# Scores by halves of 128 tokens instead of by even and odd tokens, with a new order list, in a fused recurrent-attention and bilinear feed-forward kernel

## The chip, the cores and the metric

The kernel runs on one core of a Trainium2 chip, in one launch. Time is device microseconds of one run; the median of three runs before the change is 193.85 us (193.69 to 193.97). TensorE (PE) multiplies, VectorE (DVE), ScalarE (ACT) and GpSimd (POOL) work element by element, SyncE (SP) and POOL issue nearly all transfers. Every engine takes its own instructions in the order in which they were written.

## The reference

Inputs are float32: q, k, v and alpha of 4 batches x 8 heads x 768 tokens x 48, and three weights (384x1536, 384x1536, 1536x384). A state of 48x48 per batch and head decays and grows with every token; its outputs, laid side by side over the heads, go through a bilinear feed-forward.

```python
for t in range(S):
    state = alpha[:, :, t, :, None] * state + np.einsum('bhd,bhe->bhde', k[:, :, t], v[:, :, t])
    y[:, :, t] = np.einsum('bhd,bhde->bhe', q[:, :, t], state)
...
x = y.transpose(0, 2, 1, 3).reshape(B * S, H * D)
a = x @ w_a
b = x @ w_b
return (a * b @ w_out)
```

## The kernel before

**Tiling.** A chunk is two batches (u = 0, 1) of 256 tokens; there are six (chunk c has stage c // 2 and batches c % 2 * 2 and the next). Partition p holds the token pair 2p and 2p+1 (r = 0, 1). Partitions 0 to 63 are group g = 0, 128 tokens, and 64 to 127 are g = 1. Within a group outputs come from scores (query times key, masked so that no query sees a later key); between groups and stages a state is carried (Sm, S0).

**Steps of a chunk.** Logarithms of alpha (`ln`, L556) are summed along tokens by PE (`B`, `A2` or `AQ`), ACT takes their exponentials (`E`), DVE scales keys and queries into QKp (`mk`, `mq`, L678; `lv` before them multiplies one token of each pair into the level of the other, L652, and `l2`, `l2s`, `R`, `H`, `L` prepare the sums). QKp is transposed into kqT: in chunks 0 and 1 by PE into PSUM (`C`, L736) and an eviction (`Ce`, L742, L744), from chunk 2 on by one transfer of SP for each batch (`T`, L767). `v` (vcast, L785, L787) copies the values into vxs, spaced by zeros. `K`, `K2` (L799, L812) make the states' growth, `k` (L826 to L830) adds it, `dk`, `de` or `dr`, `dl` bring the decay.

`D` (scores, L841) multiplies keys by queries. For each batch and half of the heads (h) it has 16 matmuls: per pair of heads and per key parity rk, 64 keys on the weights' side (even or odd tokens of a group) and 128 queries streamed. The four matmuls of both groups and both heads of a pair use the four quarters of PE's array together. `M` (L846) masks from PSUM into m, or `Mc` (L850, ACT) copies and `Mm` (L854, DVE) masks in place. `Y` (inner, L865) multiplies values by masked scores, 48 matmuls for a batch, again four side by side; `SB` and `SA` add what the states carry. `X` (evac, L900 on ACT, L902 on DVE) evicts a batch's y of both groups, 768 columns, to xT with the columns in the order (parity, pair). `a` and `b` (ff, L919) multiply xT by 128 columns of w_a or w_b, three matmuls for all 512 tokens of a chunk (`*`) or for 256 (0 or 1); `as` (L925, ACT) evicts a, `pr` (L933, DVE) multiplies it by b out of PSUM and puts the tokens back in their order. `o` (L941) and `oc` (L952) are the last product, `ot` evicts it, `st` stores it.

**Order.** PROGRAM (L17 to L401) is a list of such steps, chunk number first. The loop at its end (L1063 to L1068) calls them one by one, so an engine's instructions follow in the list's order. An entry's last letter is its engine (V = DVE, S = ACT, P = POOL, Y = SP), and a number for a PE step is its PSUM bank out of eight. `ld` loads, `W` and `Wo` load weights (all on POOL), `cz`, `cs`, `cm` set constants on POOL. Transfers issued by POOL take its time in line with the rest of its work. Input tiles have two buffers each, kqT and m have four, `as` three.

Of the kernel before, what the change touches and what calls it, by code (L numbers as in the profile page):

```python
# [9 lines left out]
BF16 = mybir.dt.bfloat16  # L10
# [7 lines left out]
0: cm 0; c1; cz 0 b P; ci; ld a 0b Y; c1a; ld a 0a Y; ln 0b; cu; cz 1 b P; fill 7 2; cu2 V; cz 0 q V; cus; ld k 0b Y; ld k 0a Y; B 0b 5; ld q 0b Y; ld v 0 P  # L18
0: ln 0a; ld q 0a Y; E 0b b; E 0b i; mq 0b V; B 0a 0; E 0a i; dk 0 2; E 0a b; ld a 1 P; mk 0b V; C 0 1 5; cs 0 m P; ld k 1 P; ld q 1 P; v 0 S; mk 0a V; cm 1
0: de 0; fill 2 1; mq 0a V; C 0 0 3; Ce 0 1 V; W b 0 256; cz 0 v P; Ce 0 0 V; D 0 1 4; ln 1; ld v 1 P; W a 256 768; K 0 0 6; k 0 0 V; M 0 1; D 0 0 0; SB 0 6  # L20
0: cz 1 q P; B 1a 2; M 0 0; W a 0 256; E 1a i; E 1a b; W b 256 768; mq 1a V; mk 1a V; B 1b 4; dk 1 3; E 1b i; E 1b b; de 1; v 1 S; mq 1b V; mk 1b V; C 1 0 0
0: Y 0; SA 0; Ce 1 0 V; cs 1 m P
1: ld a 0 P; ld a 1 P
0: W a 768 1536; C 1 1 1; X 0 S; c2 P; D 1 0 3; W b 768 1536
1: ld q 0 P
0: Ce 1 1 V; K 1 0 5; k 1 0 V; a 4 0 0
1: ld k 0 P
0: D 1 1 6; SB 1 1
1: ld v 0 P; ld q 1 P
0: Mc 1 0; a 3 0 5; Wo 0 6; a 0 0 3; Mm 1 0 V; Mc 1 1; as 0 0; b 0 0 4  # L30
1: ld k 1 P
0: pr 0 0; b 1 0 6; a 2 0 3; a 1 0 7; a 5 0 4; as 2 0; b 2 0 3; Mm 1 1 V; as 1 0; b 4 0 7; as 5 0; b 5 0 4; pr 2 0; pr 1 0
1: ln 0
0: SA 1; Y 1; Wo 6 12; K 1 1 6; as 3 0; as 4 0; X 1 S
1: ra 0
0: K 0 1 3
1: l2 0 V
0: b 3 0 0; pr 5 0; pr 4 0
1: H 0 V; L 0 V
0: a 2 1 1; a 5 1 2; as 5 1; pr 3 0; a 1 1 7; b 4 1 5; b 5 1 4; as 2 1; k 0 1 V; pr 5 1; a 4 1 2; as 1 1  # L40
1: ln 1
0: b 2 1 0; pr 2 1; a 6 * 3; as 4 1; b 1 1 2
1: l2 1 V
0: pr 4 1; as 6 *
1: H 1 V
0: pr 1 1
1: A2 0 7
0: a 11 * 0; a 7 * 5; a 0 1 4
1: L 1 V
0: k 1 1 V  # L50
1: ra 1
0: as 11 *
1: lv 0 q V; E 0 i
0: as 0 1; b 6 * 0; b 11 * 3; a 8 * 4; pr 6 *; pr 11 *
2: ld a * P
0: b 0 1 1; as 8 *; a 3 1 6
1: E 0 b; lv 0 k V
0: a 10 * 2; pr 0 1
1: mq 0 V; ld v 1 P
0: b 8 * 4  # L60
1: A2 1 7
0: as 10 *; b 10 * 2; pr 8 *
1: E 1 b
0: as 3 1; as 7 *; b 9 * 3; b 3 1 0; b 7 * 1; a 9 * 6
2: ld q * P
1: v 0 S; lv 1 q V; mk 0 V
0: pr 10 *
1: mq 1 V; C 0 1 4
0: as 9 *
1: C 0 0 2  # L70
0: o 0 0 5; pr 7 *
1: dk * 6
2: ld k * P
3: ld v * P
0: cz 1 v P; pr 9 *
1: Ce 0 0 S; E 1 i; de *; lv 1 k P; Ce 0 1 V; D 0 1 1; D 0 0 3
0: pr 3 1
1: Mc 0 0; K2 0 0 7 0
0: o 1 0 6
1: mk 1 V; M 0 1  # L80
0: o 3 0 4; o 1 1 -; ot 1 S; c3 P
3: ld a * P
0: cs 1 0 P; o 3 1 -
1: k 0 0 V; k 0 1 V; Mm 0 0 V; SB 0 1; C 1 0 3; C 1 1 7
0: ot 3 S; o 0 1 -
1: Ce 1 0 V
2: ln *
1: v 1 V; D 1 0 3; Ce 1 1 S; K2 1 1 6 0; Y 0; SA 0
0: ot 0 V
# [12 lines left out]
1: as 2 0
0: ot 2 S
1: pr 4 0
2: R 1; lv 1 q P
1: b 3 0 6; b 2 0 7; a 5 0 2; pr 3 0; b 5 0 3; as 5 0; b 1 0 5; a 1 0 1; pr 5 0; pr 2 0; a 7 0 2; as 1 0; pr 1 0
2: AQ 3
1: SB 1 6
2: lv 0 k P
1: a 10 0 5  # L110
2: lv 1 k V; ra 0; ld v * P
1: Mm 1 1 V
2: E 1 b
1: as 10 0; b 10 0 0; pr 10 0
2: mq 1 V; E 1 i
1: as 7 0; b 7 0 1
2: E 0 b; E 0 i
1: a 0 0 5
0: st 3 Y
2: dr  # L120
1: SA 1; Y 1
2: mk 1 V
1: pr 7 0; a 11 0 0; a 6 0 3; b 6 0 2; X 1 S; b 11 0 4; a 2 1 6; as 6 0; a 3 1 7; as 11 0; b 2 1 1; pr 6 0
2: lv 0 q V
1: b 4 1 0; as 2 1
2: T 1
1: pr 11 0
2: dl
0: st 0 Y
1: a 0 1 2; pr 2 1  # L130
2: mq 0 V
1: b 3 1 3; b 0 0 6; as 3 1; as 0 0; b 0 1 7; pr 3 1; a 8 0 1; a 9 0 5
0: st 1 Y
1: b 8 0 3; b 9 0 4; pr 0 0; as 0 1
2: mk 0 V
1: a 4 1 2
3: ln *
1: a 9 1 6; pr 0 1; as 8 0; b 9 1 1
3: ra 1
1: b 10 1 7; pr 8 0; a 10 1 3; as 4 1; as 9 0; as 9 1; a 6 1 6; b 6 1 2; b 11 1 5; pr 4 1; as 10 1; pr 9 0; a 11 1 4; pr 10 1; pr 9 1; as 6 1  # L140
2: v 1 S
1: a 8 1 3; b 8 1 1; a 7 1 6; pr 6 1
3: l2 0 V
1: as 11 1
2: T 0
1: as 8 1; a 5 1 4
3: ra 0
1: as 5 1; a 1 1 2
2: v 0 V
4: ld a * Y  # L150
1: pr 11 1; as 7 1; pr 8 1
2: K2 * * 0 7; D 1 1 3; D 1 0 5
1: as 1 1; b 5 1 2; o 2 0 1
2: k * 0 V
1: pr 5 1
3: v 0 S; v 1 S
1: b 1 1 2
2: Mc 1 0; M 1 1
3: l2s 0 P; l2s 1 P
1: b 7 1 0; o 2 1 -; pr 1 1; o 3 0 4  # L160
2: SB 0 5
# [216 lines left out]
5: b 11 * 1
# [26 lines left out]
def kernel(  # L405
# [160 lines left out]
    def bank(i):  # L566
        return psum[:, int(i)]
# [531 lines left out]
```

## Time and profile before

| | us |
|---|---|
| median of 3 runs | 193.85 (193.69 to 193.97) |
| span of the profiled execution | 192.0 |
| PE busy | 186.8 |
| DVE busy | 133.1 |
| ACT busy | 106.5 |
| POOL busy | 56.9 |
| first feed-forward matmul starts | 18.3 |
| last matmul's piece of the chain ends | 188.66 |

The span runs from the first to the last instruction; the runs' times also hold what lies around it. Matmuls are pipelined, so the mean duration of one in the profile (216 to 379 ns) is a latency; how fast they follow one another is read from their starts. PE's clock was granted in full. Lines of helpers are told apart by what they read and write.

### The profile page before, as it was taken

What the parts mean: (1) busy time and instruction counts of PE and PEld (TensorE: products, weight loads), DVE (VectorE), ACT (ScalarE), POOL (GpSimd) and SP (SyncE); (2) the same over time, 40 slices, a digit from 0 to 9 for tenths busy, and PEclk for the clock granted to TensorE, in tenths of its full rate; (3) what the DMA queues carried; (4) which work ended last, traced back from release to release, by engine and by line L of the source; (5) the groups of instructions that cost most, each with busy time, mean ns of one, the idle gap of its engine ahead of it and who ended that gap; (6) DMA issues with size and microseconds to landing.
All of it is one profiled execution on the core that took longest, in us unless ns stands there. A gap on an engine that the chain in (4) does not pass through costs nothing.

```text
span 192.0 us, 6086 instructions
## 1 busy us (share of the span) xinstructions
PE 186.8 (97%) x2613; PEld 116.9 (61%) x2613; DVE 133.1 (69%) x223; ACT 106.5 (55%) x194; POOL 56.9 (30%) x75
## 2 busy tenths in 40 slices
PE   7999999999999999999999999999999999999992
PEld 3888875677778876645557444656465644545562
DVE  2387698994989888899897956887567446252510
ACT  4448885656779867753487756743572435314211
POOL 8999626752450500640074262000000000000000
PEclk9999999999999999999999999999999999999999
DMA  5999999999969999999999989017641200000422
GB/s 132 274 219 218 251 253 235 244 269 264 251 107 166 165 216 265 248 254 149 233 213 181 156 174 129 3 42 140 146 66 44 85 0 0 0 0 3 164 82 82
DMA packets 62618, 29.40 MB, mean 153 GB/s; under 512 B 53712, under 2 KB 60768, under 8 KB 62592
## 3 DMA queue, kind: packets, MB, share of 16 engines
q0 software_dynamic: 18432, 13.37, 39.6%
q1 hardware_dynamic: 44016, 15.55, 38.1%
q8 instruction: 20, 0.33, 0.7%
q10 hardware_dynamic: 144, 0.10, 0.2%
q14 instruction: 6, 0.05, 0.1%
HBM read 25.98 MB, written 4.74 MB: 160 GB/s over the span
## 4 chain that ended last, share of the span: by engine, by line
PE 91%; DMA 5%; SPq 1%; DVE 1%; issue 1%; ACT 0%; DVEq 0%
PE psum L919 47%; PE psum L941 24%; PE psum L865 7%; PE psum L841 3%; DMA kqT<-QKp 3%; DMA q_t<-in_q_dram 3%; PE psum L736 2%; PE psum L633 1%; PE psum L952 1%; SPq L549 1%; PE psum L799 1%; PE psum L812 1%; PE psum L700 1%; PE psum L591 1%; PE psum L592 1%
## 5 line engine op out<-in xcount | busy, mean ns | idle before, releaser
L919 PE MATMUL psum<-xT,wb_t 128*128 128x512 bf16 (+1 forms) x270 | 56.0, 337 | 0.0
L919 PE MATMUL psum<-xT,wa_t 128*128 128x512 bf16 (+1 forms) x270 | 56.0, 337 | 0.0
L941 PE MATMUL psum<-wo_t,prod 128*128 128x384 bf16 x276 | 49.4, 326 | 0.0
L919 PEld LDWEIGHTS <-wb_t 128*128 128x128 bf16 x270 | 25.9, 98 | 19.9 <-issue 0.5
L919 PEld LDWEIGHTS <-wa_t 128*128 128x128 bf16 x270 | 25.9, 98 | 19.7 <-issue 0.3
L941 PEld LDWEIGHTS <-prod 128*128 128x128 bf16 x276 | 25.9, 98 | 17.6
L956 ACT ACTIVATE ot<-psum 128x384 f32<-128x384 f32 (+1 forms) x16 | 7.7, 482 | 22.7 <-PE psum L941 21.6
L850 ACT ACTIVATE m<-psum 128x1024 bf16<-128x1024 f32 x14 | 14.1, 1023 | 4.6 <-PE psum L841 4.3
L613 POOL TENSOR_TENSOR l<-la 64x384 f32<-64x384 f32 x7 | 7.8, 1108 | 26.6 <-ACT la L556 19.0
L846 DVE TENSOR_TENSOR m<-psum,mask 128x1024 bf16<-128x1024 f32 x10 | 12.1, 1220 | 3.1 <-PE psum L841 3.1
L652 POOL TENSOR_TENSOR q_t<-q_t,ra 128x384 f32<-128x384 f32 x5 | 6.1, 1215 | 22.5 <-ACT ra L645 19.7
L556 ACT ACTIVATE la<-a_t 128x1536 f32<-128x1536 f32 (+2 forms) x9 | 9.5, 1055 | 2.3 <-DMA a_t<-in_alpha_dram 2.2
L678 DVE TENSOR_TENSOR QKp<-q_t,beta 128x768 bf16<-128x768 f32 x10 | 10.0, 995 | 1.0 <-ACT beta L667 1.0
L865 PE MATMUL psum<-m,vx 64*64 64x128 bf16 x576 | 10.5, 217 | 0.0
L900 ACT ACTIVATE xT<-psum 128x768 bf16<-128x768 f32 x9 | 7.2, 816 | 5.7 <-PE psum L865 5.5
L678 DVE TENSOR_TENSOR QKp<-k_t,invb 128x768 bf16<-128x768 f32 x10 | 9.7, 972 | 0.8 <-ACT invb L667 0.8
L854 DVE TENSOR_TENSOR m<-m,mask 128x1024 bf16<-128x1024 bf16 x14 | 9.3, 684 | 1.2 <-ACT m L850 1.2
L958 DVE COPY ot<-psum 128x384 f32<-128x384 f32 (+1 forms) x9 | 4.8, 532 | 7.6 <-PE psum L941 4.7
L865 PEld LDWEIGHTS <-vx 64*64 64x64 bf16 x576 | 9.0, 107 | 0.5 <-issue 0.3
L841 PE MATMUL psum<-kqT 64*64 64x128 bf16 x384 | 9.0, 219 | 0.4 <-DMA kqT<-QKp 0.3
L652 POOL TENSOR_TENSOR k_t<-k_t,a_t 128x384 f32<-128x384 f32 x6 | 7.4, 1228 | 6.1 <-issue 3.3
L549 POOL DMA_DIRECT2D v_t<-in_v_dram x8 | 8.5, 1058 | 0.1
(271 smaller groups left out, 287.9 us busy)
## 6 DMA issues: line engine op xcount, KB each, us to landing
out_dram<-ot SPq DMA_DIRECT2D x23, 192.0 KB, 3.8
q_t<-in_q_dram SPq DMA_DIRECT2D x3, 768.0 KB, 6.5
a_t<-in_alpha_dram POOLq DMA_DIRECT2D x2, 768.0 KB, 15.2
k_t<-in_k_dram POOLq DMA_DIRECT2D x2, 768.0 KB, 12.1
v_t<-in_v_dram POOLq DMA_DIRECT2D x4, 384.0 KB, 7.0
a_t<-in_alpha_dram SPq DMA_DIRECT2D x2, 768.0 KB
k_t<-in_k_dram SPq DMA_DIRECT2D x2, 768.0 KB
a_t<-in_alpha_dram POOLq DMA_DIRECT2D x3, 384.0 KB, 8.5
```

What stands on the lines that cost most here:

```text
L549: eng.dma_start(out=t[:, us, hs].rearrange("p b h r d -> p (b h) (r d)"), in_=src[ch.b0 + us.start:ch.b0 + us.stop, hs, ch.s * 2 * C:(ch.s ...
L556: nc.scalar.activation(out=ch.la[:, us, hs].rearrange("p b h r d -> p (b h r d)"), in_=ch.a[:, us, hs].rearrange("p b h r d -> p (b h r d) ...
L613: eng.tensor_add(ch.l2[(1 - g) * HC:(2 - g) * HC, 1], x[:, :, 0, :], x[:, :, 1, :])
L652: eng.tensor_mul(x, x, by)
L678: eng.tensor_mul(QKp[ch.c % 2][:, u, j, :, hs, :D], src[:, u, hs].rearrange("p h r d -> p r h d"), f)
L841: nc.tensor.matmul(s2[g * HC:(g + 1) * HC, r, p, rk, :], lhsT=turned_part(ch, u, 1, rk, 2 * h + p, g, rs), rhs=queriesT(ch, u, 2 * h + p, ...
L846: nc.vector.tensor_mul(m.rearrange("p r a k s -> p (r a) (k s)"), ch.s2[u, h].rearrange("p r a k s -> p (r a) (k s)"), maskn(4))
L850: nc.scalar.activation(out=m.rearrange("p r a k s -> p (r a) (k s)"), in_=ch.s2[u, h].rearrange("p r a k s -> p (r a) (k s)"), func=AF.Copy)
L854: eng.tensor_mul(x, x, maskn(4))
L865: nc.tensor.matmul(y[c * DP:(c + 1) * DP, g, j // 2 * C:(j // 2 + 1) * C], lhsT=lhsT, rhs=rhs, start=(g, c) not in begun, stop=False, skip ...
L919: nc.tensor.matmul(p, lhsT=(wa_t, wb_t)[w][:, kk, f * 128:(f + 1) * 128], rhs=ch.xT[:, kk, us, :], start=(kk == 0), stop=(kk == KT - 1))
L941: nc.tensor.matmul(op, lhsT=ch.prod[:, f, at:at + C], rhs=wo_t[:, f, :], start=(f == 0), stop=(f == NFF - 1))
```

## The change

Scores are taken by the first and the last 64 tokens of a group (x = 0, 1) instead of by parity. Keys of the last 64 meet only the last 64 queries, so those matmuls stream 64 columns. m has 192 columns where it had 256, and the mask likewise. For that the 64 keys on the weights' side have to lie together. In chunks 0 and 1 PE's transposes write them so in PSUM and the eviction copies straight. From chunk 2 on a new step `Tr` (turn_keys) copies the transposed keys into a tile kp of three buffers, on ACT or DVE.

The values' rows have to stand in the same order of tokens. Half of them do already after `v`; the other half moves by 32 partitions in a new step `vs` (vswap): for a batch and a group two copies of 32 partitions x 384 elements, 13 of the 24 steps on DVE, 7 on ACT, 4 on POOL. The states' growth (`K`, `K2`) reads the loaded v instead of vxs. `X` works on one group at a time (384 columns, 10 on DVE, 14 on ACT; before it were 3 and 9 of 768) and puts the tokens in order, so that `pr` writes contiguously. The number of matmuls stays.

The whole list is new. By engine, before and after: `Ce` on DVE 6 and 4, on ACT 2 and 4; `v` on DVE 3 and 6, on ACT 9 and 6; `lv` on POOL 11 and 7, on DVE 9 and 13; `l2s` on POOL 7 and 3, on DVE 1 and 5; `l2` on DVE 6 and 5, on POOL none and 1; `ot` and `otc` on DVE 9 and 10, on ACT 16 and 15. The list's start, and the place about the middle of chunk 2, in the new order:

```
+0: C 0 0 0; Ce 0 0 V; Ce 0 1 S; ld q 1 P; K 0 0 2; de 0; k 0 0 V; D 0 1 4; ln 1; cm 1; D 0 0 0; M 0 0; W b 0 256; SB 0 2; v 0 S; vs 0 0 P; B 1a 6; E 1a b
+0: E 1a i; B 1b 0; dk 1 6; M 0 1; cz 0 v P; vs 0 1 V; Y 0; ld v 1 P; mq 1a V; mk 1a V; C 1 0 7; E 1b b; mq 1b V; W a 256 768; cz 1 q P; E 1b i; mk 1b V; SA 0
+0: X 0 1 V; X 0 0 V; C 1 1 0; Ce 1 1 V; K 0 1 1; de 1; K 1 0 6; k 1 0 V; Ce 1 0 S; D 1 0 4; Mc 1 0; k 0 1 V; b 1 0 2; a 2 0 3; W a 0 256; a 1 0 0; SB 1 4; as 1 0
+0: v 1 V; W b 256 768; as 2 0; Mm 1 0 V; pr 1 0; cs 1 m P
+1: ld a 0 P
+0: vs 1 0 V
+1: ld a 1 P
+0: W a 768 1536; vs 1 1 V; D 1 1 6; a 4 0 1; c2 P; Mc 1 1; Mm 1 1 V; b 5 0 0; b 4 0 3; a 0 0 2; as 0 0; W b 768 1536
...
+2: X 0 0 V; a 4 * 2; b 11 * 0
+3: lv 1 q P
+2: a 11 * 3; as 11 *
+4: lv 0 k V
+3: mk 0 V
+2: a 1 * 6; as 1 *; a 2 * 4
+4: ld q * Y
+2: b 2 * 3; pr 11 *
 1: ot 0 S
+3: mq 0 V; lv 1 k V; E 1 i; mk 1 V
+2: b 1 * 5; pr 1 *; a 3 * 0; a 7 * 1; as 7 *; b 7 * 6; pr 7 *; as 3 *; b 3 * 7; pr 3 *
+3: mq 1 V
+4: ra 1
 1: st 3 Y
+2: as 2 *; pr 2 *
+3: K2 * * 1 5
```

SP's transfers about there, in the old list: `T 0` of chunk 2, `ld a` of 4, `ld q` and `ld k` of 3, `ld k` of 4, a store. In the new one: `T 0` of chunk 2, `ld a` of 4, a store, `ld q` and `ld k` of 3, a store, `ld k` of 4. The functions:

```diff
     def turn(ch, u, h, i):
-        t = ch.tp[u, h] = bank(i).bitcast(BF16).rearrange("p (j r a s) -> p j r a s", j=2, r=2, a=2)
+        ch.tp[u, h] = bank(i).bitcast(BF16)
+        qs = ch.tp[u, h][:, :4 * C].rearrange("p (r a s) -> p a r s", r=2, a=2)
+        ks = ch.tp[u, h][:, 4 * C:].rearrange("p (a q r s) -> p a r q s", r=2, a=2, q=4)
...
-                    nc.tensor.transpose(t[:, j, r, p], QKp[ch.c % 2][:, u, j, r, hp:hp + 2, :].rearrange("s h d -> s (h d)"), ident)
+                    nc.tensor.transpose((ks if j else qs)[:, p, r], QKp[ch.c % 2][:, u, j, r, hp:hp + 2, :].rearrange("s h d -> s (h d)"), ident)
...
+    def turn_keys(ch, u, eng):
+        t = alloc_t(ch, u)
+        x = wk.tile([C, 8 * C], BF16, name="kp", bufs=3)
+        ch.kp[u] = x.rearrange("p (h a q w) -> p h a q w", h=2, a=2, q=4)
+        ch.qT[u] = t[:, :8 * C].rearrange("p (r h a s) -> p h a r s", h=2, a=2, r=2)
+        evict(x.rearrange("p (y r s) -> p y r s", r=2, s=HQ), t[:, 8 * C:].rearrange("p (r y s) -> p y r s", r=2, s=HQ), eng)
...
+    def vswap(ch, us, g, eng):
+        for x in range(2):
+            to, of = (slice(g * HC + n * HQ, g * HC + (n + 1) * HQ) for n in (x, 1 - x))
+            o_ = vxs[ch.c % 2][to, us, 1 - x, :, :D]
+            i_ = ch.v[of, us, :, x, :]
...
+            evict(o_, i_, eng)
...
-                        nc.tensor.matmul(kv[r * DP:(r + 1) * DP, e:e + D], lhsT=QKp[i][gs, u, 1, rk, 2 * p + r, :], rhs=vxs[i][gs, u, rk, 2 * p + r, :D], start=(rk == 0), stop=(rk == 1))
+                        nc.tensor.matmul(kv[r * DP:(r + 1) * DP, e:e + D], lhsT=QKp[i][gs, u, 1, rk, 2 * p + r, :], rhs=ch.v[gs, u, 2 * p + r, rk, :], start=(rk == 0), stop=(rk == 1))
...
+    def cols(x):
+        return slice(x * C, C + x * HC)
...
     def scores(ch, u, h, tag):
...
-            for rk in range(2):
+            for x in range(2):
...
-                        nc.tensor.matmul(s2[g * HC:(g + 1) * HC, r, p, rk, :], lhsT=turned_part(ch, u, 1, rk, 2 * h + p, g, rs),
-                                         rhs=queriesT(ch, u, 2 * h + p, g, rs), start=True, stop=True)
+                        nc.tensor.matmul(s2[g * HC:(g + 1) * HC, r, p, cols(x)], lhsT=keysT(ch, u, 2 * h + p, g, rs, x),
+                                         rhs=queriesT(ch, u, 2 * h + p, g, rs, x), start=True, stop=True)
...
+                        m = ch.m[u, h // 4][gs, h % 2 * 2 + h // 2 % 2, cols(x)].rearrange("p (r s) -> p r s", r=2)
+                        out_mm(ch, u, g, h, j, vx[gs, u, x, at:at + DP], m, x)
...
+    def evac(ch, u, g, eng):
...
+            ch.xT = wk.tile([128, B, KT, C], BF16, name="xT")
+        evict(ch.xT[:, 2 * u + g].rearrange("p a (s r) -> p a r s", r=2),
+              ch.y[u][0][:, g, :KT * C].rearrange("p (a r s) -> p a r s", a=KT, r=2), eng)
...
-            nc.tensor.matmul(p, lhsT=(wa_t, wb_t)[w][:, kk, f * 128:(f + 1) * 128], rhs=ch.xT[:, kk, us, :], start=(kk == 0), stop=(kk == KT - 1))
+            nc.tensor.matmul(p, lhsT=(wa_t, wb_t)[w][:, kk, f * 128:(f + 1) * 128], rhs=ch.xT[:, us, kk, :], start=(kk == 0), stop=(kk == KT - 1))
...
-        o_, a_, b_ = tokens(ch.prod[:, f, :], us), columns(a[:, :n], n), columns(b, n)
-        nc.vector.tensor_mul(o_, a_, b_)
+        nc.vector.tensor_mul(ch.prod[:, f, us.start * C:us.stop * C], a[:, :n], b)
```

More of the change, by code (lines that the diff above doesn't have):

```diff
@@ new lines @@
+0: ot 1 S
+2: l2s 0 V
+1: D 1 1 4; a 4 0 6; as 4 0; a 2 0 7; as 2 0
+2: l2s 1 V; R 0
+1: k 1 0 V; k 1 1 V; a 3 0 3; b 4 0 0; Mc 1 1
+2: R 1
+1: pr 4 0; a 1 0 6
+2: ra 1; lv 1 q P
+1: as 3 0
+0: ot 0 S
+1: a 5 0 7; as 5 0; b 2 0 1; pr 2 0
+2: lv 0 k V
+0: o 2 0 4
+1: SB 1 0
+2: AQ 2
+1: as 1 0
+2: E 1 b; ld v * P
+1: D 1 0 6
+2: lv 1 k P
+1: Mm 1 1 V; b 5 0 5
+2: E 1 i
+0: o 2 1 -
+2: E 0 b
+1: b 9 0 3
+2: dr
+1: M 1 0
+2: ra 0
+1: b 3 0 6; pr 5 0; b 1 0 5; SA 1
+2: mk 1 V
+1: Y 1
+2: E 0 i
+1: a 9 0 2; a 10 0 7; pr 3 0
@@ new lines @@
+1: ot 2 S
+2: D 0 0 4; Mc 0 0; D 1 0 6; Mc 1 0
+3: vs 1 1 S; l2s 0 P
+1: b 3 1 0; pr 3 1; o 0 0 1
+3: l2s 1 P; R 0
+2: SB 0 2
+3: R 1
+2: SB 1 4; D 0 1 6; Mc 0 1; Mm 0 1 V
+0: st 1 Y; cs 0 0 P
+1: o 3 0 0; o 3 1 -
+2: Mm 1 0 V
+4: ln *
+3: AQ 6; E 0 b
+4: l2s 0 P
+3: E 1 b
+2: Y 1
+3: lv 0 k P
+4: ld k * Y
+3: dr
+2: SA 1; X 1 0 S; Mm 0 0 V; Y 0; SA 0
+1: o 0 1 -
+2: X 0 1 S
+1: ot 3 S
+3: lv 0 q P
+2: X 1 1 V
+3: E 0 i
+2: X 0 0 V; a 4 * 2; b 11 * 0
+3: lv 1 q P
+2: a 11 * 3; as 11 *
+4: lv 0 k V
@@ new lines @@
+3: SA 1
+4: vs 0 0 V
+3: Y 1; X 1 1 S; Y 0; X 0 0 S
+2: o 0 0 0; o 0 1 -; o 3 1 -
+5: ln *
+3: X 0 1 V
+4: mk 0 V; T 0
+2: o 1 0 4; o 1 1 -
+3: X 1 0 V; a 0 * 2; a 8 * 3
+4: E 1 b; vs 0 1 V
+3: b 0 * 6
+5: ld k * P
+4: dr; mq 1 V; E 1 i; mk 1 V; T 1
+3: b 2 * 1
+5: l2 0 V
+3: as 0 *
+5: l2s 0 V
+4: vs 1 0 S
+3: b 3 * 2; as 8 *
+5: l2s 1 V; R 0
+4: vs 1 1 S
+3: a 3 * 3; as 3 *
+2: ot 1 S
+5: lv 0 k V
+3: pr 0 *
+1: st 1 Y
+3: b 8 * 6; pr 8 *
+2: ot 3 V
+3: a 2 * 7
+4: dl
+3: as 2 *; a 5 * 3
+4: Tr 0 S
@@ L991, in gate_t @@
     def gate_t(x, u):
[L993 removed]
+        nc.gpsimd.tensor_copy(go, x.kqT[int(u)][0:1, 0:1])
     OPS = {
```

709 lines of the change are left out of this document (281 added, 428 removed).

## Prediction

> **What bounds the kernel now.** I read the page first (totals, then the chain), then the waits of TensorE.
>
> ```profile
> span 192.0 us, 6086 instructions
> PE 186.8 (97%) x2613; PEld 116.9 (61%) x2613; DVE 133.1 (69%) x223; ACT 106.5 (55%) x194; POOL 56.9 (30%) x75
> PE 91%; DMA 5%; SPq 1%; DVE 1%; issue 1%; ACT 0%; DVEq 0%
> ...
> PE psum L574 <- DVE og L472: 1.2, 1, 1.2
> PE psum L841 <- DMA kqT<-QKp: 0.3, 1, 0.3
> PE psum L736 <- DVE QKp L678: 0.2, 1, 0.2
> ```
>
> TensorE (PE) is the chain, and after its first 9 us it waits for 0.3 us in all. So time falls by whatever work leaves PE, as long as every other engine and the loads still keep it fed. Whether they do is the question, for the order list is new from end to end. The chain's last PE piece ends at 188.66; an eviction and a store (3.3 us) follow in both kernels. The span of 192.0 lies 1.85 below the median of 193.85; I sum on the span and add 1.85 at the end. Differences within 0.2% (0.4 us) can't be told from no change.
>
> Two stages of the other engines matter. VectorE (DVE) by stretch (columns: stretch, length, busy and count of each engine):
>
> ```profile
> 40.00:60.00 20.00, 20.00 (x387) 15.18 (x380) 16.03 (x31) 13.82 (x28) 6.84 (x7) 1.00 1.16 207
> 60.00:80.00 20.00, 20.00 (x402) 14.97 (x401) 17.32 (x34) 15.32 (x29) 4.08 (x5) 1.00 1.13 220
> 80.00:110.00 30.00, 30.00 (x414) 16.11 (x413) 27.41 (x37) 18.76 (x32) 11.04 (x9) 1.00 1.05 198
> ```
>
> The third busy column is DVE: 80%, 87%, then 91%. It has little room just where keys, queries and scores of the next chunk are made beside the feed-forward. The other stage is the start, where GpSimd (POOL) issues the loads one behind the other:
>
> ```profile
> 8.50 0.77 POOL L529 DMA_DIRECT2D wb_t<-in_moe_w_b_dram  x1
> 9.32 0.74 POOL L513 MEMSET vx<- 128x768 f32 x1
> 9.99 0.90 POOL L549 DMA_DIRECT2D v_t<-in_v_dram  x1
> 10.88 0.75 POOL L529 DMA_DIRECT2D wa_t<-in_moe_w_a_dram  x1
> ...
> wb_t<-in_moe_w_b_dram POOLq DMA_DIRECT2D x1, 384.0 KB, 7.6
> ...
> v_t<-in_v_dram POOLq DMA_DIRECT2D x1, 192.0 KB, 5.5
> ```
>
> The last two lines are single issues with their us to landing: columns 256 to 768 of w_b (issued 12.86) land at 20.5, v of the second batch (issued 9.99) at 15.5. The transfer engines are full from 5 us on, so what is issued late lands late.
>
> **The change, part by part.** *PE.* Half of the scores' and half of the inner matmuls stream 64 columns instead of 128. They run four at a time, one on each quarter of the array.
>
> ```profile
> L865 PE MATMUL psum<-m,vx 64*64 64x128 bf16 x576 | 10.5, 217 | 0.0
> L841 PE MATMUL psum<-kqT 64*64 64x128 bf16 x384 | 9.0, 219 | 0.4 <-DMA kqT<-QKp 0.3
> ...
> 94.61 0.69 PE L812 MATMUL psum<-vx,QKp 64*64 64x48 bf16 x64
> 95.14 0.40 PE L841 MATMUL psum<-kqT 64*64 64x128 bf16 x16
> ```
>
> The 64 of 48 columns take 0.53 us to the next start: 33 ns for four. Four of 128 columns take 55 to 56 ns (sixteen of L841 hold the chain for 0.22 us at 100.51). For 64 columns the nearer row is 48 columns: 33 ns. Groups of four that become short: (576 + 384)/2/4 = 120. Saving 120 x 23 ns = **2.8 us**; bounds 0 (no faster than 128) and 2.9 (32 ns). The Trainium skill ("TensorE: Matmul & The Clock Gate", section "Wait — 56ns, not 53.3ns?") says that start-to-start never drops below about 25 ns however small a matmul is; then a group of four would take 100 ns and nothing would be saved. The trace disagrees for matmuls on quarters of the array: 8.3 ns each in the row above.
>
> The other matmuls keep their number. Feed-forward reads xT in runs of 128, which costs nothing: L841 already reads its queries in two runs of 64 at full rate.
>
> *DVE.* From 952 ns (xT, 768 elements) and 554 ns (ot, 384) an element of PSUM costs 1.04 ns. Ten M lose 256 elements: -2.7. Fourteen Mm (684 ns) lose a quarter at most, less the fixed part: -1.9. Ninety products write contiguously: 0 to -3, taken -1.5. X: three of 952 become ten of 0.57: +2.8. Thirteen vs, two copies each of 384 bf16 elements: 350 ns for 768 (L787) gives about 250 ns each, +6.5; bounds 4.6 (half of 350) and 14.4 (554, the rate of one element a cycle). Four Tr of 1024: +1.9 (0.35 x 1.33) to +2.8 (0.69). Work that comes over from POOL (four lv, four l2s, less one l2): +4.2; v, Ce, ot together +0.5. Sum about +9 on 133, hidden by the rest of PE's time as a total, but not where DVE stood at 91%.
>
> *ScalarE (ACT)*: 14 copies for vs at 0.49 (ot, 384) and six of 1.02 for Tr and Ce, +13; Mc, v, X and ot give back 6.5. 113 of 192 is hidden. *POOL* loses eight element-wise instructions of 1.1 to 1.2 and gains eight copies.
>
> *The start.* This is the dear part. In the list, POOL's first copy (vs 0 0 P) stands behind W b 0 256 and ahead of cz 0 v, ld v 1 and all further weights. It waits for v 0 on ACT. Before, that cast ran at 9.28. Now it stands behind Ce 0 1 (1.02), de 0 and ln 1, and ln 1 can't start before 10.80, when alpha of the second batch lands (that row stays). 10.80 + 0.84 + 0.84 = 12.4. Two POOL copies at 0.6 each (bounds 0.3, the memset of 256, and 1.2, its multiplies of 384), the memset 0.75: ld v 1 is issued at 14.3 instead of 9.99. By then all earlier loads have landed (W b 0 256 at 8.50 + 5.9 = 14.4), so nothing in the queue covers the gap. A load of two batches of v on an empty queue took 5.7 us (issued 99.37); one batch less 1.1, estimate 4.6: landing 18.9, 3.4 late (bounds 2.4 with quick copies, 4.3 with 5.5). I take 3.3, and the weights behind keep their spacing: w_b 256 to 768 lands at 23.7. The Trainium skill ("GPSIMD Engine Reference", the specifications) says that POOL shares its SBUF interfaces with VectorE; by that each copy could take the 1.2 and the start another 1.2. POOL's multiplies show 0.99 to 1.65 for one size, which agrees.
>
> PE waits meanwhile: first at K 1 0, which now reads v itself, then at a 2 0, a 1 0 and b 5 0. What it has left at b 5 0, against the old kernel where b 3 0 starts at 24.14, 164.5 before the end: seven more feed-forward halves (0.333 each), Y 1, SA 1, K 1 1, together +3.2; short matmuls still to come, -2.3. So PE ends at 23.7 + 164.5 + 0.9 = **189.1** (188.2 to 190.1) against 188.66. Without the gap it would be 185.9. The start eats the saving.
>
> *The middle.* On DVE's list, lv 0 k of chunk 4 now stands right behind the evictions of chunk 2 (free at about 80), ahead of mk 0 of chunk 3 and the product of block 11, whose bank a 3 needs. It waits for chunk 4's k, a load of SyncE (SP):
>
> ```profile
> 63.31 2.84 SPq L767 DMA_TRANSPOSE kqT<-QKp  x1
> 66.26 1.45 SPq L549 DMA_DIRECT2D a_t<-in_alpha_dram  x1
> 67.81 1.27 SPq L549 DMA_DIRECT2D q_t<-in_q_dram  x1
> 69.17 7.47 SPq L549 DMA_DIRECT2D k_t<-in_k_dram  x2
> 76.73 2.78 SPq L974 DMA_DIRECT2D out_dram<-ot  x1
> ```
>
> Four loads of 0.79 MB at the 0.26 MB/us of this stretch end at about 81. In the new list the transpose ahead of them goes about 1 later (0.5 by the list, 0.4 with PE), and two stores of 0.2 MB stand between the loads (1.5): 83.4. Then lv 0.75, mk 0.95, product 0.7: a 3 can start at 85.8. From there PE has 89 blocks of 0.656 (three of L919), 32 halves of the last product at 0.99, four at 0.5 and 10.1 of scores and states left: 102.2, and 1.8% more, by which such a sum fell short of the trace before (161.6 against 164.5 from b 3 0). 189.1 - 104.0 = 85.1. A stall of 0.5 to 0.7, and 0.3 at K2 of chunk 3, whose bank waits for pr 1: **+0.9** (0 to 2.5). Where PE, ACT and DVE hand over closely elsewhere (C 1 1 and Y 0 of chunk 1, SB 0 of chunk 1, X of chunk 2): +0.1 (0 to 1).
>
> Sum: PE ends at 190.1; +3.3 is 193.4; +1.85 is **195.3 us**.
>
> **The rivals.**
> *Faster: the late start is covered.* If v 0 runs ahead of ln 1, or the loads catch up, w_b lands by 21 and PE never waits in the start. Then 2.8 less, about 0.5 lost elsewhere: 191.6. It decides at 23.3 for w_b: earlier than that the start gains. For it: POOL is idle then, and queues that restart empty may land faster than 4.6. Against it: ACT's order is fixed and alpha's landing at 10.8 does not move. Chance 0.20.
> *Only the start costs*: k of chunk 4 lands by 82, DVE keeps up. 189.1 + 3.3 + 1.85 = 194.2, down to 193.4. Chance 0.20.
> *DVE becomes the bound from 40 to 132*: it was busy 77.5 of 92 there; nearly all the additions fall there, 87. If half of its old 14.5 idle stays, because it waits in its order, 87 + 7 = 94: 2 us more than PE has, on top of the start and of the wait for k: 198. For it: 91% in one stretch already. Against it: a late DVE finds its inputs ready. Chance 0.10.
> *The saving isn't there* (short groups take 56 ns, as by the 25 ns rule they would not shrink): 195.3 + 2.8 = 198.1. The row of 48 columns speaks against it. Chance 0.03.
>
> **How the numbers follow.** The forecast holds 0.47, with its own range 194.3 to 197.2. The range is 192.4 to 197.7: the lower end takes in most of the start's good cases, the upper the slow copies on POOL. Faster: 0.20 and a tenth of the second rival, 0.22. Same: most of the rest of that one (193.5 to 194.2), 0.13. Slower: 0.65.
>
> **What would show it.** Groups of four at 33 ns in the short scores and inner matmuls; PE busy less by about 2.8 in work. POOL idle from about 9.3 to 12.4 and ld v 1 issued near 14.3; PE waiting for loads between 17 and 24. A wait of DVE for k_t near 80 and PE waiting for a product at about 85. I am wrong if w_a and w_b are in place before PE needs them, or if DVE's row shows vs copies of 0.5 and no room left.

## The result and the profile after

The changed kernel takes 202.67 us (median of four, 201.44 to 204.85), the kernel before 193.91 beside it: a ratio of 1.042, 95% interval 1.037 to 1.047 (ratios leave out disturbed executions, so they can differ a little from the quotient of two medians). It is slower, as forecast, and by 8.8 us where 1.45 was forecast. The profiled execution is the quickest of the four, 1.2 under the median, and the account that follows is of that one. First its page, then its waits of TensorE (releaser, us in all, times, longest):

```profile
span 199.7 us, 6132 instructions
PE 188.8 (95%) x2613; PEld 116.0 (58%) x2613; DVE 141.7 (71%) x269; ACT 112.2 (56%) x215; POOL 51.4 (26%) x76
```

```profile
PE psum L829 <- DVE kp L941: 2.6, 1, 2.6
...
PE psum L903 <- DMA wa_t<-in_moe_w_a_dram: 1.1, 2, 0.6
PE psum L903 <- DMA wb_t<-in_moe_w_b_dram: 0.9, 1, 0.9
PE psum L858 <- issue: 0.7, 1, 0.7
```

TensorE's busy time rose by 2.0 although its work fell, above all because two stretches of 3.4 us each ran at half clock. The last piece of its chain ends at 196.63 instead of 188.66: 8.0 later, while the span as a whole is 7.7 longer, so all of the difference lies in that chain. To place it, I took each matmul's time from its start to the next start, and counted what exceeds the rate of its kind (216 ns for 512 columns, 163, 109 and 82 for 384, 256 and 192, 56 for a transpose, 38 for two columns, 60 for a matmul on a quarter of the array; of the first 6 us only the small matmuls). The float32 matmuls of 192 columns, which follow one another every 163 ns at full clock, are counted against 82 as well; that puts about 2 us too much into the first row, for both kernels alike:

| stretch of the span, us | before | after |
|---|---|---|
| 0 to 26 | 4.5 | 8.6 |
| 26 to 56 | 1.2 | 1.7 |
| 56 to 72 | 0.4 | 1.7 |
| 72 to 98 | 1.0 | 0.7 |
| 98 to 109 | 0.4 | 4.9 |
| 109 to 132 | 1.2 | 0.6 |
| from 132 on | 0.7 | 2.1 |
| sum | 9.4 | 20.3 |

10.9 more is lost, and 2.9 (10.9 less 8.0) saved. Where the saving is, two pieces of the chain show, the 120 inner and state matmuls of chunk 4, before and then after (start, us, matmuls):

```profile
129.08 1.80 PE psum L865 x120
```

```profile
137.68 1.51 PE psum L858 x120
```

48 of the 96 inner ones, 12 groups of four, stream 64 columns now: 0.29 / 12 = 24 ns a group, and 120 groups make 2.9. **The saving is there in full.** So is the **start**, as GpSimd's timeline (two lines) and the chain (two lines) tell it:

```profile
12.54 1.03 POOL L941 COPY vx<-v_t 32x384 bf16<-32x384 bf16 x2 [3.06 <-ACT vx L761]
...
14.31 0.90 POOL L539 DMA_DIRECT2D v_t<-in_v_dram  x1
```

```profile
17.17 6.96 DMA wb_t<-in_moe_w_b_dram
...
24.18 1.48 PE psum L903 x12
```

GpSimd stands still for 3.06 until ACT has cast v, issues the next load at 14.31, and w_b lands at 24.13. Most of the rest of the time went where no term of the forecast stood. GpSimd's timeline and SyncE's queue about the transposes of chunk 3, before:

```profile
97.16 1.00 POOL L652 TENSOR_TENSOR q_t<-q_t,ra 128x384 f32<-128x384 f32 x1 [13.30 <-ACT ra L645]
98.11 1.32 POOL L652 TENSOR_TENSOR k_t<-k_t,a_t 128x384 f32<-128x384 f32 x1
99.37 1.20 POOL L549 DMA_DIRECT2D v_t<-in_v_dram  x1
100.57 1.17 POOL L549 DMA_DIRECT2D k_t<-in_k_dram  x1
```

```profile
85.61 5.54 SPq L767 DMA_TRANSPOSE kqT<-QKp  x2
```

and after; then the second transpose as a piece of the chain, and TensorE's timeline (start, us from the first start to the last end, count):

```profile
84.81 1.20 POOL L539 DMA_DIRECT2D v_t<-in_v_dram  x1
89.83 1.16 POOL L539 DMA_DIRECT2D k_t<-in_k_dram  x1 [3.82 <-DVE prod L916]
91.37 1.15 POOL L539 DMA_DIRECT2D v_t<-in_v_dram  x1 [0.38 <-PE psum L797]
```

```profile
87.68 9.98 SPq L737 DMA_TRANSPOSE kqT<-QKp  x2
```

```profile
92.63 10.13 DMA kqT<-QKp
```

```profile
98.60 2.11 PE L924 MATMUL psum<-wo_t,prod 128*128 128x384 bf16 x12
103.27 0.37 PE L829 MATMUL psum<-kqT,kp 64*64 64x128 bf16 x16 [2.55 <-DVE kp L941]
...
105.61 2.12 PE L924 MATMUL psum<-wo_t,prod 128*128 128x384 bf16 x6
```

Before, GpSimd waited 13.3 for ACT, worked on chunk 4 and only then issued its loads, at 99.4 and later, when the transposes were through. After, those two products are VectorE's, and the two loads go out 15 and 11 us earlier, with the next load of v (112.0 before, 91.4 now) behind them, into the transposes. The second transpose lands 10.1 us after its issue, its keys are copied, and TensorE waits 2.6. Then it runs at half clock: six matmuls of 384 columns take the 2.1 us that twelve took before the wait. Wait and half clock are the 4.9 of the table. Last, the windows that answer to the three shown of before (third busy column VectorE, then ACT, GpSimd, granted clock, share and GB/s of the transfers):

```profile
40.00:60.00 20.00, 19.90 (x383) 13.96 (x382) 19.71 (x37) 16.44 (x31) 7.68 (x9) 1.00 1.31 238
60.00:80.00 20.00, 19.71 (x296) 14.86 (x296) 19.03 (x47) 17.96 (x37) 2.42 (x3) 1.00 0.95 204
80.00:110.00 30.00, 27.22 (x392) 14.12 (x392) 23.76 (x40) 15.09 (x27) 7.36 (x7) 0.94 1.23 222
```

VectorE is full from 40 to 80 (99% and 95%, where 80% and 87% stood). From 80 to 110 the granted clock is 0.94 in the mean, which is the stretch at half clock behind the transposes.

### The profile page after: what moved, and what is told of

It reads as the page before. It is cut to its first block, busy times and chain, and to the rows that moved or that the text cites. A ratio compares the mean times of both kernels' runs of the same rounds, so it can differ in the third digit from the quotient of the medians.

```text
span 199.7 us, 6132 instructions
## 1 busy us (share of the span) xinstructions
PE 188.8 (95%) x2613; PEld 116.0 (58%) x2613; DVE 141.7 (71%) x269; ACT 112.2 (56%) x215; POOL 51.4 (26%) x76
## 4 chain that ended last, share of the span: by engine, by line
PE 74%; DMA 12%; DVE 5%; POOL 4%; issue 2%; ACT 1%; POOLq 0%; DVEq 0%
PE psum L903 40%; PE psum L924 22%; DMA kqT<-QKp 5%; PE psum L858 5%; DMA wb_t<-in_moe_w_b_dram 3%; DMA a_t<-in_alpha_dram 3%; DVE prod L916 2%; PE psum L829 2%; DVE QKp L668 1%; PE psum L623 1%; PE psum L935 1%; PE psum L797 1%; PE psum L728 1%; POOL v_t L539 1%; DVE vx L941 1%
## 5 line engine op out<-in xcount | busy, mean ns | idle before, releaser
L924 PEld LDWEIGHTS <-prod 128*128 128x128 bf16 x276 | 26.6, 99 | 18.9 <-issue 1.3
L903 PEld LDWEIGHTS <-wa_t 128*128 128x128 bf16 x270 | 25.2, 97 | 20.3 <-DMA wa_t<-in_moe_w_a_dram 1.6
L842 ACT ACTIVATE m<-psum 128x768 bf16<-128x768 f32 x14 | 11.1, 810 | 9.4 <-PE psum L829 9.4
L939 ACT ACTIVATE ot<-psum 128x384 f32<-128x384 f32 (+1 forms) x15 | 7.0, 469 | 10.9 <-PE psum L924 10.2
L939 ACT ACTIVATE xT<-psum 128x384 bf16<-128x384 f32 x14 | 7.6, 609 | 7.3 <-PE psum L858 7.3
L838 DVE TENSOR_TENSOR m<-psum,mask 128x768 bf16<-128x768 f32 x10 | 9.4, 951 | 0.6 <-PE psum L829 0.6
L846 DVE TENSOR_TENSOR m<-m,mask 128x768 bf16<-128x768 bf16 x14 | 8.4, 609 | 0.5 <-ACT m L842 0.5
L941 DVE COPY ot<-psum 128x384 f32<-128x384 f32 x10 | 5.3, 552 | 4.5 <-PE psum L924 4.5
L941 POOL COPY vx<-v_t 32x384 bf16<-32x384 bf16 x8 | 4.3, 538 | 15.9 <-DVE vx L763 10.7
L858 PE MATMUL psum<-kqT,Sm 64*64 64x128 bf16 x144 | 7.7, 220 | 0.7 <-issue 0.7
L603 POOL TENSOR_TENSOR l<-la 64x384 f32<-64x384 f32 x3 | 3.0, 994 | 20.4 <-issue 10.8
L858 PE MATMUL psum<-m,vx 64*64 64x64 bf16 (+1 forms) x576 | 8.2, 205 | 0.0
L941 DVE CAST xT<-psum 128x384 bf16<-128x384 f32 x10 | 5.7, 586 | 3.4 <-PE psum L858 3.4
```

The lines of the kernel that those rows point to most:

```text
L838: nc.vector.tensor_mul(m, x, maskn())
L842: nc.scalar.activation(out=m, in_=x, func=AF.Copy)
L846: eng.tensor_mul(m, m, maskn())
L858: nc.tensor.matmul(o, lhsT=lhsT, rhs=rhs, start=(g, c) not in begun, stop=False, skip_group_check=True)
L903: nc.tensor.matmul(p, lhsT=(wa_t, wb_t)[w][:, kk, f * 128:(f + 1) * 128], rhs=ch.xT[:, us, kk, :], start=(kk == 0), stop=(kk == KT - 1))
L924: nc.tensor.matmul(op, lhsT=ch.prod[:, f, at:at + C], rhs=wo_t[:, f, :], start=(f == 0), stop=(f == NFF - 1))
```

## The experiments

All ratios are against runs of the kernel before on the same chip, in brackets the 95% interval; "above before" is the ratio less one, times 194 us. The changed kernel is 8.1 above by that measure.

**The start.** e1_start:

```diff
-vs 0 0 P; B 1a 6
+vs 0 0 V; B 1a 6
```

> The changed kernel with one engine letter altered: the first swap of the first batch (vs 0 0) is made by VectorE instead of GpSimd, so that GpSimd's queue no longer stands still from 9.5 to 12.5 us. Theory 'the start costs what the late loads cost': v of the second batch is issued near 10 instead of 14.3, w_b 256:768 lands near 20 instead of 24.1, the three waits for weights at 20.1, 21.1 and 23.0 (2.4 us in the trace) go, and the time falls by about 2.4 (1.5 to 4) from 202.7. Rival 'what sets the start is TensorE itself, held at half clock from 12 to 15.2': the weights come early, but TensorE reaches them no earlier, and the time falls by less than 0.7.

199.1 us, 1.026 (1.021 to 1.030): 5.0 above, 3.1 gained. v of the second batch was issued at 10.21, w_b landed at 20.22, and of the waits for weights one of 0.3 is left. The theory holds, but a part of the gain is the clock: e1_start's profile has no half clock in the start, where the changed kernel has it from 12.3 to 15.5. e8_pool, below, has the same start with half clock from 12 to 15; counted as in the table it loses 7.1 up to 26 us, against 4.9 in e1_start and 8.6 in the changed kernel. The stall at the transposes stayed (2.7).

**The transposes: the loads, or VectorE's lateness.** e2_gate puts a GpSimd copy of one element of the transposed tile ahead of the loads, e3_lvk moves VectorE's product that waits for k behind the four products of chunk 3:

```diff
+3: gatet 1
 4: ld v * P; v 0 V
```

```diff
-4: lv 0 k V
 3: mk 0 V
...
 3: mq 1 V
+4: lv 0 k V
```

> The changed kernel with one GpSimd instruction added, a copy of one element that waits until the second DMA transpose of chunk 3 has landed, ahead of the loads of v of chunk 4 and of k and v of chunk 5 (issued at 84.8, 89.8 and 91.4, while the two transposes run from 87.7 to 102.8). Theory 'the transposes are slow because these loads share the transfer engines': each transpose lands within 6 us again, the second before 99, TensorE's wait at 100.4 (2.9 us) and the half clock behind it (1.7) go, and the time falls by about 4.6 (3 to 5). Rival 'the transposes are late because VectorE is late': they still land near 102, no change beyond 1.

> The changed kernel with VectorE's first product on chunk 4 (lv 0 k, which waits 1.73 us for k at 84.4) moved behind the four keys and queries products of chunk 3. Theory 'the transposes are late because VectorE waits for k ahead of the products they need': the first transpose is issued near 85.9 instead of 87.7, the second is 1 to 2 us earlier than 92.6, TensorE's wait at 100.4 shrinks from 2.9 to about 1.2, and the time falls by 1.7 to 3.4. Rival 'contention alone': the second transpose still takes 10 us to land behind the loads of v and k, time within 1 of the changed kernel's.

> Both edits, the loads held back until the transposes have landed and lv 0 k moved behind the products. If either cause alone suffices, the time is that of the better of the two alone; if the two add, the wait at 100.4 and the half clock behind it are gone and the time is about 4.6 to 5.5 below the changed kernel's (197 to 198). If the stall has a third cause (the order on SyncE's queue, the copy of the keys behind the transpose), it stays above 1 us here.

e2_gate: 198.9, 1.024 (1.021 to 1.027), 4.6 above: 3.5 gained. The transposes took 3.01 and 1.95 us of SyncE's queue again, the wait and the half clock at 100 were gone. e3_lvk: 205.9, 1.055 (1.048 to 1.062): no gain, 2.5 worse. Its transposes took 11.6 us from the first issue, TensorE waited 4.2 for the copied keys. The first transpose went out at 89.39, right behind mq 0, and mq 0 stood behind the product of block 11, which waited 0.92 for ACT's eviction of TensorE's result and not for k. But TensorE itself was late in this run: its profile lost 2.9 at once to weights in the start, though nothing was changed there, and ran at half clock until 27.5; that part isn't explained. So the run shows the slow transposes again without a wait for k ahead of them, and doesn't price that wait. e4_both: 1.026 (1.016 to 1.035), an interval too wide to tell it from e2_gate. For the stall at 100 the loads are the cause; that VectorE's wait for k adds to it isn't shown.

The same cause, put into the kernel before (b1_early):

```diff
-4: ld v * P
...
-5: ld k * P; l2s 0 P
+5: l2s 0 P
...
+4: ld v * P
+5: ld k * P
 5: ld a * Y
```

> The kernel before, with nothing of the change in it, and its two GpSimd loads of v of chunk 4 and k of chunk 5 (issued at 99.4 and 100.6) put ahead of GpSimd's two products of chunk 4, as early as they stand in the changed kernel (about 84 to 91). Theory 'loads of 0.4 to 0.8 MB beside the transposes are what slows these': the two transposes of chunk 3 take 4 to 5 us of SyncE's queue each instead of 3.0 and 1.9, land 8 to 10 us after their issue, and TensorE waits 0 to 2 us for them near 98 to 101; the time is 0 to 3 more than before. Rival 'the transposes of the changed kernel are slow for what stands in its own queue': the transposes keep 3.0 and 1.9, time unchanged within 0.3.

198.6, 1.025 (1.023 to 1.028): 4.9 slower, more than the 0 to 3 expected. SyncE's queue, GpSimd's first load and TensorE's first line of waits:

```profile
85.73 11.29 SPq L768 DMA_TRANSPOSE kqT<-QKp  x2
```

```profile
83.92 1.20 POOL L550 DMA_DIRECT2D v_t<-in_v_dram  x1
```

```profile
PE psum L842 <- DMA kqT<-QKp: 2.7, 2, 1.7
```

Two loads moved ahead in GpSimd's queue, nothing else, and the pair of transposes takes 11.3 us instead of 5.5. Of the 4.1 us that its span grew, 2.7 are waits for the transposed tile itself, and 0.9 is a wait for a cast of v on ACT.

**Both mends together, and what the parts are worth.** e5_two is e1_start and e2_gate in one. e8_pool has e1_start's edit too, and holds the loads back much as the kernel before did, by GpSimd's work, with three products of chunk 4 ahead of them:

```diff
-4: lv 1 q V
+4: lv 1 q P
...
-4: lv 1 k V
+4: lv 1 k P
...
-4: ld v * P; v 0 V
...
-4: AQ 0; E 0 b; lv 0 q V; v 1 V; mq 0 V
+4: AQ 0; E 0 b; lv 0 q P; ld v * P; v 0 V; v 1 V; mq 0 V
```

e6_wide and e7_noswap start from e5_two. e6_wide streams 128 columns in every score and inner matmul, so that scores and outputs hold other values; e7_noswap leaves out the steps vs, so that half of the values stand at the wrong tokens (the edit shown is e6_wide's):

```diff
-nc.tensor.matmul(s2[g * HC:(g + 1) * HC, r, p, cols(x)], lhsT=keysT(ch, u, 2 * h + p, g, rs, x),
-                 rhs=queriesT(ch, u, 2 * h + p, g, rs, x), start=True, stop=True)
+nc.tensor.matmul(s2[g * HC:(g + 1) * HC, r, p, x * C:(x + 1) * C], lhsT=keysT(ch, u, 2 * h + p, g, rs, x),
+                 rhs=queriesT(ch, u, 2 * h + p, g, rs), start=True, stop=True)
...
-out_mm(ch, u, g, h, j, vx[gs, u, x, at:at + DP], m, x)
+out_mm(ch, u, g, h, j, vx[gs, u, x, at:at + DP], m)
```

> The changed kernel with the two edits that helped: the first swap on VectorE, and the loads of chunks 4 and 5 held back until the transposes of chunk 3 have landed. Theory 'two separate causes, at 20 us and at 100 us': the two gains add, 202.7 - 3.6 - 3.8 = 195.3 (194.3 to 196.3), neither a wait for weights above 1 us nor a wait for the copied keys is left. Rival 'one shared queue, so that curing the first brings the second back': the start runs 3 us earlier, meets other transfers, and the sum of the gains is under 6.

> The kernel of e5_two with the short matmuls streaming 128 columns again, as many matmuls as before: scores and inner matmuls of the last 64 tokens go over all 128 columns, so that y and the scores hold other values. It prices the saving. Theory 'short groups of four save 24 to 28 ns each and TensorE is the bound': 120 groups, 2.9 to 3.4 more than e5_two. Rival 'the saving is hidden behind VectorE or the loads': less than 1 more.

> The kernel of e5_two without any of the swapped copies of v (the output of the inner part is then of other tokens). VectorE, ACT and GpSimd lose 26, 14 and 8 copies (7.5, 7.3 and 4.3 us of the trace). Theory 'the engines beside TensorE have become too full between 54 and 72, where TensorE waits three times for a product (1.2 us in all)': 1 to 2 us less than e5_two. Rival 'the copies are hidden': within 0.5.

> The changed kernel with the first swap on VectorE and, in place of the wait, three of chunk 4's element-wise products given back to GpSimd (lv 1 q, lv 1 k, lv 0 q) ahead of the load of v. Theory 'GpSimd issues the loads into the transposes because the change took its work away': v of chunk 4 and k of chunk 5 are issued near 95 to 98 by themselves, the second transpose lands within 7 us, TensorE's wait for the copied keys goes, and the time equals e5_two's within 1, less if VectorE's relief counts. Rival 'only an explicit wait holds the loads': the loads still start near 87, the wait stays near 3, time near 199.

e5_two: 1.009 (1.006 to 1.013), 1.8 above: 6.3 gained of the 6.6 that the two gained alone. They are separate causes. e8_pool: 196.2, 1.011 (1.008 to 1.014). GpSimd's timeline shows the loads kept back by its own product, and the transposes took 2.97 and 1.95:

```profile
95.07 0.99 POOL L641 TENSOR_TENSOR q_t<-q_t,ra 128x384 f32<-128x384 f32 x1 [3.44 <-ACT ra L634]
96.01 1.21 POOL L538 DMA_DIRECT2D v_t<-in_v_dram  x1
```

e6_wide: 196.8, 1.014 (1.012 to 1.017), only 0.9 more than e5_two where 2.9 to 3.4 were expected. So about a third of the saving comes out in the time, though the two intervals leave 0 to 1.8 for that difference. e7_noswap: 194.0, 0.999 (0.995 to 1.002), 2.1 less than e5_two: the copies cost 2.1 (1.1 to 3.1 by the intervals) where the short matmuls save TensorE 2.9. Its excess from 56 to 72 us is 0.7, where e5_two has 1.6 and the changed kernel 1.7.

**What is next.** e9_warm puts `warm 12 6` ahead of `B 1a 6` in e5_two. e10_idle and e11_idle2 move sixteen swapped copies (chunks 2 and 3) to GpSimd, on top of e9_warm and, with e8_pool's edit, without the wait.

> The kernel of e5_two with twelve small matmuls on zeros (128 columns, 0.67 us at full clock, into a bank that the next cumulative sum overwrites) put where TensorE idles from 11.2 to 12 us for the logarithms of the second batch. Theory 'that idle costs the clock: 0.7 to 0.9 us without work, and TensorE runs at half clock for 3.4 us or more': the granted clock is 1.0 in every run, the span stays near 193.6 (the e5_two runs at clock 1.0), the time near 195.4 with a spread under 1, instead of 195.3 to 198.6. Rival 'the half clock is set by something else': still 0.98 to 0.99 in some runs, and the median unchanged within 0.5 at 196.6.

> The kernel of e9_warm with the swapped copies of chunks 2 and 3 (sixteen copies) made by GpSimd, which is idle from 57 to 80 us, instead of VectorE and ACT. Theory 'the copies cost where VectorE is full, not in themselves': TensorE's small waits between 54 and 72 shrink from 1.6 to about 1, and the time is 0.5 to 1.3 less than e9_warm. Rival 'GpSimd's copies, twice as long (0.50 against 0.25), come too late or slow VectorE': 0 to 1.5 more than e9_warm.

> As e10_idle, but with the products given back to GpSimd (e8_pool) in place of the explicit wait. If the relief of VectorE between 85 and 110 counts, 0.3 to 1 less than e10_idle; if not, the same within 0.3. Whether either falls below the kernel before (194.1) is open: e10_idle by the sum of the two theories would be 194.1 to 194.9.

e9_warm: 196.9 (196.1 to 197.4), 1.015 (1.013 to 1.017). The granted clock was 0.998 to 1.0 in all five executions, as expected, but the time did not fall; it is 1.1 above e5_two. VectorE and TensorE at 84:

```profile
84.47 0.56 DVE L643 TENSOR_TENSOR k_t<-k_t,a_t 128x384 f32<-128x384 f32 x1 [4.58 <-DMA k_t<-in_k_dram]
```

```profile
86.54 1.46 PE L904 MATMUL psum<-xT,wa_t 128*128 128x512 bf16 x6 [1.68 <-DVE prod L917]
```

Now TensorE is there in time, and the wait for k of chunk 4 stops it. That is the state of this one profile: two executions of e5_two that had the full clock without the twelve matmuls took 195.3 and 195.6, and why e9_warm is slower than those isn't shown. e10_idle and e11_idle2: 1.017 (1.014 to 1.020) and 1.015 (1.013 to 1.017), nothing gained. The waits at 54 to 72 shrank, but GpSimd's sums for chunk 3 came late, as e11_idle2 shows on VectorE:

```profile
75.81 0.96 DVE L612 TENSOR_TENSOR lh<-l 128x768 f32<-128x768 f32 x1 [1.63 <-POOL l L602]
```

**k of chunk 4, and the rest.** e13_key moves its load, e14_lvk is e9_warm with e3_lvk's edit, e15_pool is e13_key with e8_pool's edit for the wait, e16_wide is e13_key with 128 columns throughout:

```diff
 3: ld q * Y; ld k * Y
+4: ld k * Y
...
-4: ld k * Y
 3: dr
```

> The kernel of e9_warm with the load of k of chunk 4 put ahead of the store that stands before it on SyncE's queue (4.5 us of that queue at 72.6). Theory 'a third cause, the load's place': k is issued near 73 and lands near 81 instead of 84.5, VectorE's wait shrinks from 4.6 to under 1.5, TensorE's wait at 84.5 (1.7 to 2.1) goes, and the time is 1.2 to 2 less than e9_warm (195.0 to 195.7). Rival 'the transfer engines are full there and k lands no earlier': less than 0.5.

> The kernel of e9_warm with VectorE's product on k of chunk 4 moved behind the products of chunk 3 (the edit of e3_lvk, which brought nothing while the start was late). Theory 'the wait counts only once TensorE comes on time': TensorE's wait at 84.5 goes and the time is 1 to 2 less than e9_warm (195 to 196). Rival 'VectorE's own list is the limit': less than 0.5.

> The kernel of e13_key with the products given back to GpSimd in place of the explicit wait. By what e8_pool and e5_two showed, the same within 0.5 of e13_key; if VectorE's relief of 2 us in that stretch counts now, 0.5 to 1 less (194.0 to 194.7), which would be at the kernel before.

> The kernel of e13_key with the short matmuls streaming 128 columns (other values in the scores and in y). With the granted clock at 1.0 in both it prices the saving: 2.8 to 3.3 more than e13_key if TensorE is the bound throughout; e6_wide against e5_two at clock 1.0 showed 1.2 in span. If it is again near 1.2, half or more of the saving is lost to waits of other engines that the longer matmuls cover.

e13_key: 196.1, 1.010 (1.007 to 1.013), VectorE's wait for k 1.8 instead of 4.6. e14_lvk: 195.4, 1.009 (1.006 to 1.013). Both are about 1 below e9_warm (0.9 and 1.1, the first a little under what was expected), and TensorE's wait at 84 is gone in both. The edit that brought nothing in e3_lvk counts in e9_warm; against e5_two (1.8 above) neither gains anything. e15_pool: 196.6, 1.012 (1.008 to 1.016), no difference between the two ways to hold the loads. e16_wide: 197.1, 1.016 (1.013 to 1.020), 1.2 more than e13_key (0.2 to 2.2 by the intervals), again less than half of 2.9 at the middle of its interval.

Two attempts at all mends together (for k that of e14_lvk), e17_best and e18_best2 (both with `2: vs 1 0` and `2: vs 1 1` on P; the second with `Mc 1 0` and a later `Mm 1 0 V` for `M 1 0` of chunk 1):

> All mends together: first swap on VectorE, twelve filling matmuls, chunk 4's products on GpSimd ahead of its loads, k's product of chunk 4 moved behind chunk 3's, and four copies (the second batch of chunk 2) on GpSimd in place of VectorE. Theory 'the copies ahead of the products are the rest': TensorE's wait at 66 (0.57) goes, nothing new comes, and the time is 194.0 to 195.0. Rival 'every copy moved turns up at another engine': 195 to 196.5.

> The kernel of e14_lvk with the same four copies on GpSimd, and one masked eviction of chunk 1 (M 1 0, 0.95 us of VectorE ahead of a product) split into an eviction by ACT and a masking in place behind that product. Theory: the waits at 56 (0.37) and 66 (0.57) both go, 0.6 to 1.0 less than e14_lvk (194.3 to 194.9). Rival: they move to the inner matmuls behind, same within 0.4 (195.0 to 195.8).

e17_best: 195.9, 1.010 (1.008 to 1.012). e18_best2: 196.2, 1.010 (1.007 to 1.013). The wait at 66 halved (0.57 to 0.29) and others grew. No version of the change that keeps the whole computation beat the kernel before; the best are 1.8 to 2.0 above it.

## Why the forecast went the right way and fell short, step by step

- **PE's saving of 2.8**: right, 2.9, at 24 ns a group. The rule of the Trainium skill ("TensorE: Matmul & The Clock Gate", "Wait — 56ns, not 53.3ns?") of at least 25 ns from start to start doesn't hold for these: a long and a short group of four take 88 ns together where two long ones take 112, so about 32 ns are left for the four matmuls of a short one. Reading xT in runs of 128 cost nothing, as said: 216 ns from start to start for 512 columns in both kernels.
- **The engines' sums**: right. DVE 141.7 for about 142 (the terms listed add up to about 10, not 9; 8.6 came), ACT 112.2 for 113. A vs copy took 250 on DVE at the median and 287 in the mean, 520 on ACT, 500 to 540 on POOL.
- **The start**: right in place and mechanism. ld v 1 at 14.31 (14.3 said), v landed at 18.17 (18.9), w_b 256 to 768 at 24.13 (23.7). The loss from 0 to 26 is 4.1, where 189.1 against 185.9 put 3.2; the mend gained 3.1. That TensorE would fall to half clock there was not foreseen; in the changed kernel most of it is hidden, since the weights come later still.
- **k of chunk 4, +0.9 at a 3**: the load was as late as said (VectorE got k at 84.4, 83.4 said) and VectorE waited 1.7, but TensorE waited 0.3 there at most. The late start and the small waits behind it had moved TensorE by more than the term's margin. In e9_warm, with those mended, the wait appeared (1.7 to 2.1), and its two cures gained 1 there.
- **The step that failed** is the line "POOL loses eight element-wise instructions of 1.1 to 1.2 and gains eight copies". It was costed as time on POOL and nothing else. POOL's queue also holds loads: two products of chunk 4 that went to DVE (lv 1 q and lv 1 k) had stood ahead of the loads of v and k, the first of them waiting 13.3 for ACT, and had kept these loads out of the transposes. That is 4.5 of the 6.5 us by which the forecast's end of PE, 190.1, was too early. e2_gate, e8_pool and b1_early show it from three sides. The direction did not hang on it: with this stall alone mended (e2_gate) the kernel is still 4.6 slower.
- **DVE as the bound** was a rival with 0.10 and is a part of the truth: full from 40 to 80, it cost TensorE 1.3 between 56 and 72, which the +0.1 for close handovers elsewhere did not cover.
- **Left open**: in the changed kernel and in the variants one matmul at the end of the run of inner and state matmuls near 150 to 160 starts 0.6 to 1.2 us late, 0.9 in the changed kernel, with no wait that the profile shows (the line `issue` among TensorE's waits), and not in the kernel before. The traces narrow it down: in all 18 kernels with the new list it is TensorE's 2397th matmul, also in the nine with twelve matmuls more ahead, where that is another matmul of the list; and it starts 1.2 to 1.6 us behind the end of a packet of an instruction queue (q8, 20 packets of 16 KB). In the two kernels with the old list the packet before that matmul had ended 4.1 and 4.6 us earlier. That points at the supply of TensorE's instructions in a fast run of small matmuls; no experiment was aimed at it. Nor is it settled where the rest of the saving goes, more than half of it, that e6_wide and e16_wide don't give back; the waits that mends laid bare one by one (k, VectorE's products, GpSimd's sums) suggest that the order list has little room left at any of them.

## What to carry to other kernels

When work leaves an engine that also issues transfers, list the transfers queued behind it: they will start earlier, and what they meet then must be costed like any other step. A stall that a trace doesn't show may stand right behind another one (the wait for k, seen in e9_warm alone); mend the first before calling the second harmless. A saving on the bounding engine is worth what the other engines leave of it, here 0.9 and 1.2 of 2.9 by two pairs of runs, so price the work that buys it (2.1 us of copies) against that and not against the whole.

## What the runs showed of the hardware

- **DMA transposes beside loads.** The same two transposes took 3.04 and 1.93 us of SyncE's queue (before), 3.01 and 1.95 (e2_gate), 2.97 and 1.95 (e8_pool) with no GpSimd load beside them, and 4.86 and 5.03 (after), 5.06 and 6.14 (b1_early) with loads of v and k beside them. The Trainium skill ("DMA: Bandwidth & Descriptors", "Issuing engines are not separate DMA queues") says that transfers of all issuing engines run on the same sixteen and interleave; the runs agree, and give the price for these transposes: the pair takes 9.9 to 11.2 instead of 5.0.
- **The clock falls after little idling.** After the wait of 2.6 us that ended at 103.3 the matmuls from 104.4 to 107.7 ran at half rate. In the start, delays of 0.4, 0.2 and 0.75 us from one matmul's start to the next, between 10.1 and 11.8, were followed by half rate from 12.3 to 15.5. With 0.39 in place of the 0.75 (e1_start), or twelve small matmuls in its place (e9_warm), there was no half rate at 12; with 0.48 (e2_gate) there was. The edit does not settle it: e8_pool and e5_two have e1_start's start, and in their profiles 0.68 and 0.88 stood there, with half clock until 15 and until 18.
